# A recurrence before a router: state products moved behind the next scores, rank and logit products moved within the turn

## The chip, the cores and the metric

The kernel runs on one core of a Trainium2 chip. Its engines work side by side: TensorE (PE in the profile; its weight loads are PEld), VectorE (DVE), ScalarE (ACT), GpSimd (POOL), and the DMA queues that SyncE (SP) and GpSimd feed. Each engine takes its instructions in program order and waits for others through semaphores. The metric is the device time of one execution in microseconds (us).

## The reference

Two stages, all in float32. First a linear recurrence with decay (batch 4, 8 heads, 768 steps, 48 wide):

```python
for t in range(S):
    kt, vt, rt = (k[:, :, t], v[:, :, t], r[:, :, t])
    cur = np.einsum('bhd,bhe->bhde', u[None] * kt, vt)
    y[:, :, t] = np.einsum('bhd,bhde->bhe', rt, state + cur)
    state = w[None, :, :, None] * state + np.einsum('bhd,bhe->bhde', kt, vt)
```

Its output, as 3072 rows of 384 numbers, goes to a router with 8 experts: cosine logits of each row against 8 expert vectors, the best expert and its softmax weight, and then `gate * (relu(x @ w1[e]) @ w2[e])` with w1 384 x 1024 and w2 1024 x 384.

## The kernel before

The recurrence is done in chunks of 128 steps. A *unit* i is one chunk c of one batch row b (`c, b = divmod(i, 4)`), so there are 24 units, and one turn of the loop handles one unit, with parts of its neighbours. Four units make a *group* of the router. Within a chunk, y is the sum of three things: the state from before the chunk times r (`T`, `RT`), the masked scores within the chunk times v (`AT`, `V`), and the diagonal with u (`xd`, on ScalarE). Heads go in pairs, 48 rows each at partitions 0 and 64.

```python
def turn_r(k, i):      # TensorE: four transposes (rt), DVE: RT = rt * powers of the decay
def turn_k(k, i):      # TensorE: four transposes (kt), ScalarE: KT = copy of kt

def scores(k, i):
    RT, KT = k.RT[i], k.KT.pop(i)
    at = [k.ps.tile([128, NP, C], F32, name="at", tag="at") for _ in range(2)]
    for p in range(NP):
        for s in range(2):
            rows = slice(s * DP, s * DP + D)
            nc.tensor.matmul(at[s][:, p, :], KT[rows, p, :], RT[rows, p, :], start=True, stop=True)   # L388

def masked(k, i, s):   # DVE: AT[s] = at[s] * umask                                                   # L394
def states(k, i):      # TensorE: st = K^T V of this chunk                                            # L409
def carry(k, i):       # DVE, GpSimd: state += st, state *= decay of a chunk

def sums(k, i):
    ...
    y = [k.ps.tile([128, NP // 2, C], F32, name="y", tag="y") for _ in range(2)]
    for q in range(NP // 2):
        for u in range(2) if c > 0 else ():
            for s in range(2):
                p, n = 2 * q + u, (DP, D)[u]
                mm(                                                                                   # L443
                    y[s][u * DP : u * DP + n, q, :], T[s * DP : s * DP + D, p * D : p * D + n],
                    RT[s * DP : s * DP + D, p, :], start=(q == 0), stop=False, skip_group_check=True,
                )
    for s in range(2):
        for q in range(NP // 2):
            for u in range(2):
                ...
                mm(                                                                                   # L452
                    y[s][u * DP : u * DP + n, q, :], V[:, h * D : h * D + n], AT[s][:, p, :],
                    start=(c == 0 and q == 0), stop=True, skip_group_check=True,
                )
        yT = k.yT[i % len(k.yT)]
        nc.scalar.copy(yT[0:PP, s], y[s][0:PP])                                                       # L457

def rows(k, i):        # TensorE: four transposes of yT (yrows, L470), DVE: X = yrows + xd (L476)
def own_rows(k, i, half):  # ScalarE: four of the eight xd = V * diag (L346)
def turn_rows(k, g, b):    # TensorE: three transposes of X (xp, L556), ScalarE: xT = copy of xp (L558)
def squares(k, g, b):      # ScalarE: sum of squares of X (L563)
def logits(k, g):          # TensorE: lgT, 12 products with 32 columns (L572); needs the xT of four units
def logits_out(k, g):      # ScalarE: copy of lgT
def turn_logits(k, g):     # TensorE: one transpose (lg)
def ranks(k, g):           # TensorE: two products (rank, L625, L626); DVE reads them in places
def located(k, g):         # DVE: two small operations on what places gives
def taken(k, g):           # TensorE: four products (take, L718)
```

PSUM's eight banks are handed out by tag, in turn:

```python
HELD = {"tp": (0, 1), "at": (2, 3), "y": (4, 5), "st": (6,), "xp": (7,), "ps": (0, 1, 6, 7, 2, 3, 4, 5)}
```

rt, yrows, lgT and rank share the two banks of "tp"; each unit's y takes both banks of "y". The loop, cut to the steps that matter, in the order in which each engine gets them:

```python
for i in range(-1, units):
    ...
    whole(places, i - 4)           # whole(f, n): only when n is the last unit of a group
    whole(logits_out, i - 3)
    on(turn_r, i + 1)              # rt
    on(own_rows, i, 0)             # xd, first half
    on(turn_k, i + 1)              # kt, KT
    whole(turn_logits, i - 3)
    ...                            # scaled, own (GpSimd), squares, own_rows(i, 1), choose, before
    whole(located, i - 4)
    ...                            # gates, lanes, listed, own_sum
    on(sums, i)                    # L443, L452, yT
    on(states, i)                  # st
    whole(taken, i - 6, "xp")
    on(carry, i)
    on(scores, i + 1)              # at
    on(masked, i + 1, 0)
    on(rows, i)                    # yrows, X
    on(masked, i + 1, 1)
    of_group(put, i)               # X to memory
    of_group(turn_rows, i - 1)     # xp, xT
    whole(logits, i - 2)           # lgT
    whole(ranks, i - 3)            # rank
```

In the last turns two tiles of rows for the two smallest experts are gathered early (`Early`): the list for it is worked out on DVE, a gather on GpSimd brings the rows, and `turn` transposes them (early_x, L1025) after the last unit's sums. The rest of the experts follows as one long run of matmuls.

Of the kernel before, what the change touches and what calls it, by code (L numbers as in the profile page):

```python
# [10 lines left out]
F32 = mybir.dt.float32  # L11
# [6 lines left out]
B, H, S, D = 4, 8, 768, 48  # L18
DM, E, F = H * D, 8, 1024
N = B * S  # L20
C = 128
NCH = S // C
DP = 64
NP = H // 2
# [211 lines left out]
def build_experts(k):  # L236

    nc, pool = k.nc, k.aconst
    emb, tau = k.emb_rows, k.tau_rows
    sq = k.work.tile([E, DM], F32, name="emb_sq", tag="sq")  # L240
    nrm = pool.tile([E, 1], F32, name="emb_nrm")
    nc.scalar.activation(sq, emb, ACT.Square, accum_out=nrm)
    nc.gpsimd.tensor_tensor(out=nrm, in0=nrm, in1=k.half[0:E, 0:1], op=ALU.pow)
    nc.gpsimd.tensor_scalar(nrm, nrm, 1e-6, tau, ALU.add, ALU.mult)
    yield
    nc.vector.reciprocal(nrm, nrm)
    yield
    nc.scalar.mul(emb, emb, nrm)
    yield
    ps = k.ps.tile([128, NK, E], F32, name="ps", tag="xp")  # L250
    for c in range(NK):
        nc.tensor.transpose(ps[:, c, :], emb[:, c * 128 : (c + 1) * 128], k.ident[0:E, 0:E])
    nc.vector.tensor_copy(k.ent[:, :, 0:E], ps)
    yield
# [19 lines left out]
def load_w1(k, e, w1):  # L274
    k.nc.sync.dma_start(out=w1, in_=k.w1[bass.ds(e, 1)].rearrange("o (c p) f -> p (o c) f", p=128))
# [59 lines left out]
def own_sum(k, i):  # L335
    diag = k.work.tile([128, H], F32, name="diag", tag="diag")
    k.nc.vector.reduce_sum(diag, k.KU.pop(i), axis=AX.X)
    k.diag[i] = diag
# [53 lines left out]
def masked(k, i, s):  # L392
    a = k.work.tile([128, NP, C], F32, name=f"AT{s}", tag=f"AT{s}")
    k.nc.vector.tensor_mul(a, k.at[i][s], k.umask[:, None, :].to_broadcast([128, NP, C]))  # L394
    k.AT.setdefault(i, []).append(a)
# [29 lines left out]
    nc.gpsimd.tensor_mul(T[0:PP], T[0:PP], k.wC[0:PP])  # L425


def sums(k, i):

    nc = k.nc
    mm = nc.tensor.matmul
    c, b = divmod(i, B)
    V, RT, AT, T = k.loaded[i][2], k.RT.pop(i), k.AT.pop(i), k.state[b]
    V, T = (a.rearrange("q h d -> q (h d)") for a in (V, T))
    y = [k.ps.tile([128, NP // 2, C], F32, name="y", tag="y") for _ in range(2)]
    for q in range(NP // 2):
        for u in range(2) if c > 0 else ():  # L440
            for s in range(2):
                p, n = 2 * q + u, (DP, D)[u]
                mm(  # L443
                    y[s][u * DP : u * DP + n, q, :], T[s * DP : s * DP + D, p * D : p * D + n],
                    RT[s * DP : s * DP + D, p, :], start=(q == 0), stop=False, skip_group_check=True,
                )
    for s in range(2):
        for q in range(NP // 2):
            for u in range(2):
                p, n = 2 * q + u, DP if c == 0 and u == 0 else D  # L450
                h = 2 * p + s
# [6 lines that stand above are left out]
    if b == 0:  # L458
        k.groups[c] = group(k, c)
# [77 lines left out]
def group(k, c):  # L537

    g = Net()
    g.c = c  # L540
    g.X = k.rows.tile([128, B, DM], F32, name="X", tag="X")
    g.ssq = k.rt.tile([128, B], F32, name="ssq", tag="ssq")
    g.xT = {}
    return g
# [92 lines left out]
def norms(k, g):  # L637
    k.nc.gpsimd.tensor_tensor(out=g.ssq, in0=g.ssq, in1=k.half, op=ALU.pow)
# [72 lines left out]
def listed(k, g):  # L711
    g.what = chosen(k, g.c, g.sel)
# [134 lines left out]
def attention(k):  # L847


    units = B * NCH  # L850

    def on(f, i, *more):
        if 0 <= i < units:
            f(k, i, *more)

    def of_group(f, i):
        if 0 <= i < units:
            f(k, k.groups[i // B], i % B)

    def whole(f, i, *more):  # L860
        if 0 <= i < units and i % B == B - 1:
            f(k, k.groups[i // B], *more)

    emb, tables = build_experts(k), build_turned(k)
    for i in range(-1, units):
        j = i - SETTLED * B
        if 0 < i + AHEAD < units:
            load(k, i + AHEAD)
        whole(places, i - 4)
        whole(logits_out, i - 3)  # L870
        if i >= 0:
            on(turn_r, i + 1)
        if i == 0:
            own_sum(k, i)
        if B <= i < units - 1:
            on(own_rows, i, 0)
        if i >= 0:
            on(turn_k, i + 1)
        if 0 < i < B:
            own_rows(k, i, 0)  # L880
        whole(turn_logits, i - 3)
        if i == B + 3:
            norms(k, k.groups[0])
        on(scaled, i + 2)
        if i < 0:
            own_r(k, 0)
        on(own, i + 2)
        for n in SQUARES.get(i, (i - 1,)):
            of_group(squares, n)
        if B <= i < units - 1:  # L890
            on(own_rows, i, 1)
        if i > B + 1:
            whole(norms, i - 2)
        if j == 10:
            k.lists = turned_lists(k, perm, "tp")
            lists = taken_by_rank(k, k.lists)
            first = [Early(k, r, *lists, w) for r, w in zip(LAST, k.weights)]
        whole(choose, i - 3)
        whole(before, i - 3)
        whole(located, i - 4)  # L900
        whole(gates, i - 5)
        whole(lanes, i - 5)
        whole(listed, i - 5)
        if 0 <= i < units - 2:
            on(own_sum, i + 1)
        if j == 7:
            load_, count = loads(k, "xp")
        if j == 9:
            expert_of(k, by)
            number = expert_number(k, LAST[0])  # L910
            load_w1(k, number, k.weights[0][0])
        on(sums, i)
        on(states, i)
        for n in (0, 1) if i == 0 else (1,) if 0 < i < B else ():
            own_rows(k, i, n)
        whole(taken, i - 6, "xp")
        whole(exps, i - 4)
        on(carry, i)
        if 0 < i < B + 2:
            next(tables)  # L920
        whole(summed, i - 6)
        if i == B:
            next(emb)
        on(scores, i + 1)
        on(masked, i + 1, 0)
        if i == 0:
            masked(k, i + 1, 1)
        if i == units - 1:
            first[0].turn()
        on(rows, i)  # L930
        if i != 0:
            on(masked, i + 1, 1)
        if i == units - 2:
            own_sum(k, i + 1)
            own_rows_once(k, i + 1)
        of_group(put, i)
        if j == 10:
            load_w2(k, number, k.weights[0][1])
        of_group(turn_rows, i - 1)
        whole(logits, i - 2)  # L940
        whole(ranks, i - 3)
        if i == 0:
            build_constants(k)
        if i in (1, 2, 3):
            next(emb)
        if 3 <= i < 3 + len(k.ring):
            k.nc.gpsimd.memset(k.ring[i - 3], 0.0)
        if j == 8:
            by = order(k, load_)
        if j == 9:  # L950
            settle(k, by, count)
            perm = turner(k, by)


    g, h = k.groups[NCH - 2], k.groups[NCH - 1]
    early = itertools.chain(*(f.steps(lambda: to) for f in first))

    def fill(count):
        for _ in range(count):
            next(early, None)  # L960

    load_weights(k, expert_number(k, LAST[1]), k.weights[1])
    first[1].turn()
    fill(1)
    gates(k, g)
    lanes(k, g)
    listed(k, g)
    turn_rows(k, h, B - 1)
    squares(k, h, B - 1)
    norms(k, h)  # L970
    fill(1)
    logits(k, h)
    logits_out(k, h)
    fill(1)
    turn_logits(k, h)
    choose(k, h)
    before(k, h)
    to = outs(k, lists[0], E * TM)
    taken(k, g, "tp")
    fill(2)  # L980
    ranks(k, h)
    load_, _ = loads(k, "xp")
    places(k, h)
    exps(k, h)
    located(k, h)
    lanes(k, h)
    gates(k, h)
    listed(k, h)
    summed(k, g)
    by = order(k, load_, k.settled)  # L990
    perm = turner(k, by)
    fill(6)
    taken(k, h, "tp")
    summed(k, h)
    fill(1)
    lists = turned_lists(k, perm, "xp")
    k.take, k.gates = taken_by_rank(k, lists)
    k.rows_of = {r: gathers(k, r) for r in LAST}
    k.to = outs(k, k.take, E * TM)
    caps_passed(k, load_, by)  # L1000
    for _ in early:
        pass
# [615 lines left out]
```

## Time and profile before

The time before is 398.59 us, the median of 3 runs (398.39 to 399.5); the profiled execution has a span of 396.4 us, with the full clock granted to TensorE (0.997).

| engine | busy us | share of the span |
|---|---|---|
| TensorE matmuls | 386.9 | 98% |
| TensorE weight loads | 352.5 | 89% |
| VectorE | 253.2 | 64% |
| ScalarE | 173.1 | 44% |
| GpSimd | 160.9 | 41% |

The loop over the units takes roughly the first 131 us, the experts the rest. In the loop ScalarE is far busier than over the span: 7.0 to 8.0 us of each 10 us from 40 to 120 us.

How to read the lines: a line of the timeline gives the start in us, the duration from the first start to the last end, the engine, the line of the kernel, the operation, what is written from what, the shape (rows*columns of the array for matmuls), and how many records. In brackets stands the idle time of the engine just before it and what ended it. A float32 matmul is recorded as two passes, so eight products are sixteen records. Matmuls overlap by their pipeline depth: a group's first start to the next group's first start is the time that it takes. In the view of one tile, a line says which engine's instruction waited for it, for how long in sum, and how often.

### The profile page before, as it was taken

What the parts mean: (1) busy time and instruction counts of PE and PEld (TensorE: products, weight loads), DVE (VectorE), ACT (ScalarE), POOL (GpSimd) and SP (SyncE); (2) the same over time, 40 slices, a digit from 0 to 9 for tenths busy, and PEclk for the clock granted to TensorE, in tenths of its full rate; (3) what the DMA queues carried; (4) which work ended last, traced back from release to release, by engine and by line L of the source; (5) the groups of instructions that cost most, each with busy time, mean ns of one, the idle gap of its engine ahead of it and who ended that gap; (6) DMA issues with size and microseconds to landing.
All of it is one profiled execution on the core that took longest, in us unless ns stands there. A gap on an engine that the chain in (4) does not pass through costs nothing.

```text
span 396.4 us, 9266 instructions
## 1 busy us (share of the span) xinstructions
PE 386.9 (98%) x3542; PEld 352.5 (89%) x3542; DVE 253.2 (64%) x600; ACT 173.1 (44%) x524; POOL 160.9 (41%) x216
## 2 busy tenths in 40 slices
PE   7999999999999999999999999999999999999993
PEld 4988888889888877899999999999999999799783
DVE  6887878787788670757667668257275456655601
ACT  4887777777677412333333332233323243133120
POOL 7998796858664232500701502220350350200111
PEclk9999999999999999999999999999999999999998
DMA  7899887767606972244705532434164170150111
GB/s 146 163 215 214 189 180 162 157 136 149 142 33 206 288 285 65 87 161 163 255 7 215 196 106 94 133 112 161 55 227 159 43 237 3 40 180 0 41 39 44
DMA packets 93797, 54.35 MB, mean 137 GB/s; under 512 B 76938, under 2 KB 88381, under 8 KB 93747
## 3 DMA queue, kind: packets, MB, share of 16 engines
q1 hardware_dynamic: 90242, 44.26, 41.4%
q0 software_dynamic: 3296, 9.44, 7.3%
q8 instruction: 29, 0.48, 0.5%
q14 instruction: 22, 0.17, 0.1%
q10 hardware_dynamic: 208, 0.00, 0.0%
HBM read 44.45 MB, written 9.63 MB: 136 GB/s over the span
## 4 chain that ended last, share of the span: by engine, by line
PE 86%; SPq 4%; ACT 3%; DMA 2%; DVE 2%; POOL 1%; issue 1%; POOLq 0%; DVEq 0%; ACTq 0%
PE ps L1226 25%; PE ps L1290 18%; PE ps L1330 5%; PE at L388 4%; PE ps L1344 4%; PE y L452 4%; PE early_h L1036 3%; PE early_y L1045 3%; PE ps L1204 3%; PE yrows L470 2%; PE ps L1174 2%; PE y L443 2%; PE rt L360 2%; PE kt L369 2%; PE xp L556 2%; PE st L409 2%
## 5 line engine op out<-in xcount | busy, mean ns | idle before, releaser
L1090 POOL DMA_INDIRECT out_dram<-y,to x25 | 30.1, 1204 | 173.5 <-DVE Sh L1365 109.9
L1226 PE MATMUL ps<-xTe,w 128*128 128x192 f32 (+3 forms) x336 | 62.9, 327 | 0.0
L1226 PEld LDWEIGHTS ps<-xTe,w 128*128 128x128 f32 x336 | 55.9, 190 | 0.5
L346 ACT ACTIVATE xd<-V,diag 128x48 f32<-128x48 f32 x184 | 46.2, 326 | 0.1
L394 DVE TENSOR_TENSOR AT<-at,umask 128x512 f32<-128x512 f32 x48 | 32.7, 685 | 10.5 <-PE at L388 10.3
L1233 ACT ACTIVATE hT<-hT 128x384 f32<-128x384 f32 (+3 forms) x42 | 22.0, 523 | 32.4 <-DVE hT L1256 19.7
L1290 PE MATMUL ps<-Tw,Sh 128*128 128x192 f32 x192 | 32.5, 326 | 0.0
L1290 PEld LDWEIGHTS ps<-Tw,Sh 128*128 128x128 f32 x192 | 31.4, 190 | 0.0
L1081 POOL DMA_INDIRECT G<-xs,take x25 | 27.0, 1080 | 10.5 <-issue 4.6
L1226 PE MATMUL ps<-Tx,Sw 128*128 128x192 f32 (+3 forms) x168 | 29.7, 326 | 0.0
L388 PE MATMUL at<-RT,KT 48*128 48x128 f32 x384 | 27.9, 285 | 0.3 <-DVE RT L362 0.3
L1243 DVE TENSOR_TENSOR u<-ps,p 128x384 f32<-128x384 f32 (+3 forms) x14 | 7.8, 558 | 31.3 <-ACT p L1240 16.6
L1226 PEld LDWEIGHTS ps<-Tx,Sw 128*128 128x128 f32 x168 | 27.6, 190 | 0.1
L452 PE MATMUL y<-AT,V 128*48 128x128 f32 (+1 forms) x384 | 26.0, 278 | 0.0
L388 PEld LDWEIGHTS at<-RT,KT 48*128 48x128 f32 x384 | 23.3, 187 | 2.6 <-issue 0.7
L332 POOL TENSOR_TENSOR KU<-KU,Rpad 128x384 f32<-128x384 f32 x24 | 24.1, 1004 | 1.8
L452 PEld LDWEIGHTS y<-AT,V 128*48 128x48 f32 (+1 forms) x384 | 19.9, 124 | 4.2 <-issue 3.6
L1290 PE MATMUL ps<-w,hT 128*128 128x192 f32 x128 | 23.4, 326 | 0.0
L328 POOL TENSOR_TENSOR KU<-K,u_bc 128x384 f32<-128x384 f32 x23 | 23.2, 1008 | 0.0
L317 POOL TENSOR_TENSOR Kpad<-K,kpow 128x384 f32<-128x384 f32 x23 | 23.1, 1004 | 0.1
L558 ACT COPY xT<-xp 128x384 f32<-128x384 f32 x24 | 11.5, 479 | 25.5 <-PE xp L556 25.5
L1253 ACT ACTIVATE hT<-ps 128x384 f32<-128x384 f32 (+3 forms) x14 | 6.9, 490 | 35.7 <-PE ps L1226 35.7
(240 smaller groups left out, 816.5 us busy)
## 6 DMA issues: line engine op xcount, KB each, us to landing
w<-in_moe_w_dram SPq DMA_DIRECT2D x16, 1536.0 KB, 6.9
Rpad<-in_r_dram SPq DMA_DIRECT2D x24, 192.0 KB, 4.4
V<-in_v_dram SPq DMA_DIRECT2D x24, 192.0 KB, 4.2
xs<-X SPq DMA_DIRECT2D x24, 192.0 KB, 2.7
K<-in_k_dram SPq DMA_DIRECT2D x23, 192.0 KB, 3.7
G<-xs,take POOLq DMA_INDIRECT x27, 3.2
out_dram<-y,to POOLq DMA_INDIRECT x25, 3.5
Kpad<-in_k_dram SPq DMA_DIRECT2D x1, 192.0 KB, 3.2
```

What stands on the lines that cost most here:

```text
L317: k.nc.gpsimd.tensor_mul(k.Kpad[i % len(k.Kpad)][:, :, 0:D], k.loaded[i][0], k.kpow)
L328: k.nc.gpsimd.tensor_mul(k.KU[i], k.loaded[i][0], k.u_bc)
L332: k.nc.gpsimd.tensor_mul(k.KU[i], k.KU[i], k.loaded[i][1][:, :, 0:D])
L346: k.nc.scalar.mul(k.xd[i][:, h, :], V[:, h, :], diag[:, h : h + 1])
L388: nc.tensor.matmul(at[s][:, p, :], KT[rows, p, :], RT[rows, p, :], start=True, stop=True)
L394: k.nc.vector.tensor_mul(a, k.at[i][s], k.umask[:, None, :].to_broadcast([128, NP, C]))
L452: mm(y[s][u * DP : u * DP + n, q, :], V[:, h * D : h * D + n], AT[s][:, p, :], start=(c == 0 and q == 0), stop=True, skip_group_check=True,)
L1081: nc.gpsimd.indirect_dma_start(out=G[0:n, :], out_offset=None, in_=k.xs[:, :], in_offset=IndirectOffsetOnAxis(ap=take[0:n], axis=0), bound ...
L1090: put = k.nc.gpsimd.indirect_dma_start(out=k.out[:, :], out_offset=IndirectOffsetOnAxis(ap=to, axis=0), in_=y, in_offset=None, bounds_chec ...
L1226: nc.tensor.matmul(ps[:, j, :], weights[:, (f + j) * 128 : (f + j + 1) * 128], moving, start=(first and j == 0), stop=True, skip_group_che ...
L1233: nc.scalar.activation(h, h, ACT.Relu)
L1290: nc.tensor.matmul(ps, a[:, f, :], b[:, f, :], start=(first and f == 0), stop=(f == NF // 2 - 1), skip_group_check=True)
```

## The change

The products with the state are taken out of `sums` into a step of their own, `from_state`, which the loop runs for the next unit, right behind that unit's scores. The two have the same 48 rows, at partitions 0 and 64, and both read RT. The two masks then follow one another on DVE, ahead of the X of the unit before. The products for the ranks move from the end of a turn to the middle of the next turn, with the operations that read them; there the bank that they leave is not wanted at once. The logits move from the end of a turn to just in front of V's products of the same turn, both being products with 128 rows and few columns, and ScalarE's copy of them follows in the same turn. The same instructions are run, in another order.

```diff
-def sums(k, i):
+def from_state(k, i):
     c, b = divmod(i, B)
-    V, RT, AT, T = k.loaded[i][2], k.RT.pop(i), k.AT.pop(i), k.state[b]
-    V, T = (a.rearrange("q h d -> q (h d)") for a in (V, T))
-    y = [k.ps.tile([128, NP // 2, C], F32, name="y", tag="y") for _ in range(2)]
+    RT, T = k.RT.pop(i), k.state[b].rearrange("q h d -> q (h d)")
+    y = k.y[i] = [k.ps.tile([128, NP // 2, C], F32, name="y", tag="y") for _ in range(2)]
     for q in range(NP // 2):
         for u in range(2) if c > 0 else ():
             ...
+def sums(k, i):
+    V, AT, y = k.loaded[i][2].rearrange("q h d -> q (h d)"), k.AT.pop(i), k.y.pop(i)
     for s in range(2):
         ...
@@ the loop
-        whole(places, i - 4)
-        whole(logits_out, i - 3)
         ...
-        whole(located, i - 4)
         ...
             on(own_sum, i + 1)
+        for step in (ranks, places, located):
+            whole(step, i - 4)
         ...
+        whole(logits, i - 2)
         on(sums, i)
+        whole(logits_out, i - 2)
         on(states, i)
         ...
         on(scores, i + 1)
-        on(masked, i + 1, 0)
-        if i == 0:
-            masked(k, i + 1, 1)
+        on(from_state, i + 1)
+        for s in range(2):
+            on(masked, i + 1, s)
         ...
         on(rows, i)
-        if i != 0:
-            on(masked, i + 1, 1)
         ...
         of_group(turn_rows, i - 1)
-        whole(logits, i - 2)
-        whole(ranks, i - 3)
```

More of the change, by code (lines that the diff above doesn't have):

```diff
@@ L425, in carry @@
     nc.gpsimd.tensor_mul(T[0:PP], T[0:PP], k.wC[0:PP])
+def from_state(k, i):
+    c, b = divmod(i, B)
+    RT, T = k.RT.pop(i), k.state[b].rearrange("q h d -> q (h d)")
+    y = k.y[i] = [k.ps.tile([128, NP // 2, C], F32, name="y", tag="y") for _ in range(2)]
+    for q in range(NP // 2):
+        for u in range(2) if c > 0 else ():
+            for s in range(2):
+                p, n = 2 * q + u, (DP, D)[u]
+                k.nc.tensor.matmul(
+                    y[s][u * DP : u * DP + n, q, :], T[s * DP : s * DP + D, p * D : p * D + n],
+                    RT[s * DP : s * DP + D, p, :], start=(q == 0), stop=False, skip_group_check=True,
+                )
 def sums(k, i):
@@ L435, in sums @@
     c, b = divmod(i, B)
-    V, RT, AT, T = k.loaded[i][2], k.RT.pop(i), k.AT.pop(i), k.state[b]
-    V, T = (a.rearrange("q h d -> q (h d)") for a in (V, T))
-    y = [k.ps.tile([128, NP // 2, C], F32, name="y", tag="y") for _ in range(2)]
[L439 to L446, printed above, removed]
+    V, AT, y = k.loaded[i][2].rearrange("q h d -> q (h d)"), k.AT.pop(i), k.y.pop(i)
     for s in range(2):
@@ L924, in attention @@
         on(scores, i + 1)
-        on(masked, i + 1, 0)
-        if i == 0:
-            masked(k, i + 1, 1)
+        on(from_state, i + 1)
+        for s in range(2):
+            on(masked, i + 1, s)
         if i == units - 1:
```

## The prediction

> **What bounds the kernel now.** I read the busy shares first, then the stage by 10 us windows, then the timelines of TensorE and of ScalarE over one turn of the attention loop, and last the tile that ties the two together.
>
> The page says that TensorE is busy 98% of the span and weight loads 89%. So time is lost or won only where the chain on TensorE gets longer or shorter. The loop over the 24 units (one chunk of 128 steps of one batch row each) runs from about 8 to 131 us; the experts after it hang on its end.
>
> One plain turn, from the timelines of TensorE and its weight loads:
>
> ```profile
> 69.12 0.49 PE L556 MATMUL xp<-ident,X 128*128 128x128 f32 x3
> 69.45 0.60 PE L360 MATMUL rt<-ident,Rpad 128*128 128x128 f32 x4
> 69.89 0.60 PE L369 MATMUL kt<-ident,Kpad 128*128 128x128 f32 x4
> 70.42 0.66 PE L443 MATMUL y<-RT,state 48*64 48x128 f32 x16
> 71.00 1.08 PE L452 MATMUL y<-AT,V 128*48 128x128 f32 x16
> 71.91 0.61 PE L409 MATMUL st<-V,Kpad 128*64 128x48 f32 x16
> 72.46 1.16 PE L388 MATMUL at<-RT,KT 48*128 48x128 f32 x16
> 73.55 0.60 PE L470 MATMUL yrows<-ident,yT 112*128 112x112 f32 x4
> 73.99 0.49 PE L556 MATMUL xp<-ident,X 128*128 128x128 f32 x3
> ...
> 70.42 0.41 PEld L443 LDWEIGHTS y<-RT,state 48*64 48x64 f32 x16 [0.17 <-issue]
> 71.00 0.82 PEld L452 LDWEIGHTS y<-AT,V 128*48 128x48 f32 x16 [0.17 <-issue]
> ```
>
> The groups follow without a hole: from xp to xp is 73.99 - 69.12 = 4.87 us, and that is TensorE's own work. Before L443 (48*64) and L452 (128*48) the weight loads pause 0.17 us with nothing to wait for: the shape of the array changes there, as it does at L388 (48*128) and L470 (112*128). The same turn on ScalarE:
>
> ```profile
> 69.65 0.48 ACT L558 COPY xT<-xp 128x384 f32<-128x384 f32 x1 [1.34 <-PE xp L556]
> 70.03 1.01 ACT L346 ACTIVATE xd<-V,diag 128x48 f32<-128x48 f32 x4
> 70.94 0.56 ACT L378 COPY KT<-kt 128x512 f32<-128x512 f32 x1
> 71.40 0.53 ACT L563 ACTIVATE sq<-X 128x384 f32<-128x384 f32 x1
> 71.83 0.19 ACT L563 ACTIVATION_READ_ACCUMULATOR sq<-X 128x1 f32 x1
> 71.92 1.00 ACT L346 ACTIVATE xd<-V,diag 128x48 f32<-128x48 f32 x4
> 72.82 0.62 ACT L457 COPY yT<-y 112x256 f32<-112x256 f32 x2
> 74.52 0.48 ACT L558 COPY xT<-xp 128x384 f32<-128x384 f32 x1 [1.07 <-PE xp L556]
> ```
>
> ScalarE works without a hole from xT at 69.65 to the end of yT at 72.82 + 0.62 = 73.44: 3.79 us. Then it idles 1.07 us, until TensorE has done yrows (which reads yT) and xp (which stands behind yrows). So there is a ring: yT, then yrows and xp on TensorE, then xT and all the rest on ScalarE, then the next yT. Here yT ends at 73.44 and yrows starts at 73.55: the ring is only 0.1 us shorter than TensorE's own work. ScalarE is busy 78% of such a turn, and yet has nearly no room. Three turns already show it (the tile yT, who waited for it):
>
> ```profile
>   PEld yrows L470: 0.9, 3
> ```
>
> **What the Trainium skill says.** (1) "TensorEngine Tiling (Array Packing)", Key Properties: changing the tiling mode drains TensorE. The trace agrees: the first matmul of a new mode starts 0.20 us after the last one of the old, against 0.10 to 0.11 us inside a group, for each change here, also where only the columns change (xp to lgT, 0.20). (2) "TensorE: Matmul & The Clock Gate", the opening table: ScalarE's queue is strict FIFO. The trace agrees: xT is in front of xd, KT, sq and yT in every turn, and all of them lie idle while xT waits for xp. (3) "PSUM — Partial Sum Buffer", PSUM bank collisions raise a hardware error: a bank must be guarded by semaphores between engines. y has two banks and each unit takes both, so a product into y must wait until ScalarE has copied the y of the unit before. In the program as built, the moved products do carry a wait for ScalarE. (4) "Perfetto Trace Analysis", Optimizing Tensor Performance: matmul groups should rotate through PSUM banks so that evacuation of one lies beside the next. Here that rotation has a depth of one for y; no run so far shows more.
>
> **The change part by part.** No instruction is added or removed; TensorE's order changes, DVE and ScalarE move a few.
>
> *Products with the state (L443), from in front of V's products (L452) to behind the next scores (L388).* By modes: before kt, L443, L452, st, at, yrows has four changes (into 48*64, into 128*48, into 48*128 after st, into 112*128); after, kt, L452, st, at, L443, yrows has four again (into 128*48, 48*128, 48*64, 112*128). At 0.14 us each (0.20 instead of 0.11, and about 0.05 for the weights that could not be loaded ahead) that is a gain of nothing, unless a change of columns alone between at and L443 costs nothing, which xp to lgT speaks against.
>
> By waits: L443 of unit i+1 now writes y right after the scores, and so waits for both copies yT of unit i. And it stands between yT and yrows. The ring gets longer: yT end to first L443 0.05 (as at yrows where it waited, 116.7), L443 0.39, change 0.20, yrows 0.34, xp 0.10 + 0.22, last xp start to xT 0.31 (69.34 to 69.65): 1.61 us, and ScalarE's 3.79: 5.40 us. Before it was 1.61 - 0.39 - 0.20 = 1.02 and 3.79: 4.81. TensorE's work stays 4.87. So a plain turn goes from 4.87 to 5.40: +0.53.
>
> *Logits in front of V's products.* Before, xp, lgT, rt costs two changes of mode; after, kt, lgT, L452 replaces the change kt to L452, so one less: 0.14 per group of four units. ScalarE's copy of lgT moves into its idle time. The turn with lgT (0.79 more) and take (0.45 more) is 4.87 + 0.79 + 0.45 = 6.11 on TensorE, longer than the ring.
>
> *Ranks a turn later.* Before, rt behind the rank products starts 0.30 us after the last of them and goes on at 0.165 instead of 0.11: it waits for a bank that DVE's X add frees. That is 0.47 - 0.22 = 0.25 us per group; it goes away. After, the turn with ranks has 4.87 + 0.36 = 5.23 on TensorE, below the ring's 5.40.
>
> *One group of four turns, steady.* Before (starts of L443 at 48.83 and 70.42, 91.999, ...): 21.58 us. After: 6.11 + 3 x 5.40 = 22.31. So +0.73 per group, with the savings of ranks and logits counted in: without the ring they would have given -0.39.
>
> *The sum.* I place y443 of unit 4 where yrows of unit 3 stood (24.94) and compare each later one with the yrows of the unit before.
> - Units 4, 5, 6: ScalarE has two squares instead of one (and emb), passes of 4.80, 4.30, 4.30, with 1.60 each: 6.40, 5.90, 5.90, ending at 43.14 against 41.62: +1.5. Unit 7: 5.40 against 5.48: +1.4 in sum.
> - Units 8 to 19: three groups, +0.69 each by the exact starts (66.93 against 64.87): +3.5 in sum.
> - Unit 20 (no st any more): 5.40 against 4.55: +4.3. Unit 21, TensorE-bound with lgT (4.38 + 0.79 + 0.43 = 5.60) against 4.93: +5.0; part of that is lgT moved forward, and would come back in unit 22.
> - It does not come back: early_x at 130.79 waits for a gather, whose list is worked out on DVE behind the scores of unit 22 (at ends 121.5, gather issued 125.60, landed 130.65). That chain starts +5.0 late, so early_x stands at 135.8, and TensorE, ready at about 134.7, waits some 1.1 us there instead of 0.6.
> From early_x to the end TensorE is full and unchanged: +5.0 us, 398.6 to 403.6. I take 403.4, as a few small waits may overlap.
>
> **The rivals.**
> A. *Only TensorE counts, and the change does what it is for.* For it: TensorE 98% busy, ScalarE only 44% of the span and with an idle time of over 1 us each turn. Then 4 rank waits x 0.25 and 5 logits x 0.14 give -1.7 us: 396.9; part lost again at the gather, which would then come last: 397.8. Against it: that idle time is itself a wait for TensorE, and the margin of yT is 0.1 us in the plain turns (0.5 in those with more on TensorE).
> B. *The change from at to L443 is free, as both have rows of 48.* Then 20 x 0.14 = 2.8 us more would be saved: 395. Against it: xp to lgT shares its rows too, and pays 0.20. And with the ring last, TensorE's saving is worth nothing in three turns of four.
> C. *DVE becomes the bound*: the X add now stands behind both masks, and yrows comes later. DVE is 4.68 of 4.87 us busy in the fullest turn (69.65 to 74.52). A turn of 5.40 leaves it 0.7 us, so I hold it off the path; if RT came late for the scores, some 0.2 us per turn more: up to 407.
> D. *ScalarE's pass gets shorter*: y is ready earlier, but yT waits for ScalarE's own queue, not for y (its products end at about 72 us, yT starts at 72.82). No gain.
>
> **Range and chances.** The main term, 0.53 to 0.7 us for some 14 turns, rests on two intervals measured in the trace and on one wait that is in the program. What is unsure is the start (+-1), the tail (+-1) and C. Predicted 403.4 us, 400.5 to 406.5 eight times in ten. Two per cent faster (390.6) is beyond even B: 0.02. Two per cent slower (406.6) needs C or a longer tail: 0.10. Within 2%: 0.88.
>
> **What would show it.** In the profile after: L443's weight loads wait for ACT yT, about 0.5 us in three turns of four, where before yrows waited three times in all; a plain turn of 5.4 us; ScalarE's idle before xT rises from 1.07 to about 1.6 us; no wait at rt behind ranks; lgT with one pause less; early_x later by about 5 us, and the experts as long as before. I am wrong if plain turns stay at 4.87 (then yT is not waited for, A or B), or if the waits before L443 name DVE (C).

## The result, and the profile after

The changed kernel takes 403.02 us (median; 402.74 to 403.27), against 398.59 before. The ratio is 1.0109, 95% interval 1.0094 to 1.0123: it is slower by 1.1%, or 4.4 us. The profiled execution has a span of 401.0 us against 396.4, and the engines' counts of instructions are the same.

The busy shares hardly show it. From the page after:

```profile
PE 389.8 (97%) x3542; PEld 354.7 (88%) x3542; DVE 253.5 (63%) x600; ACT 171.9 (43%) x524; POOL 162.2 (40%) x216
```

TensorE has 2.9 us more recorded as busy, and every share went down a point. It is the single turn that tells. The timeline of TensorE after, one plain turn (no logits, ranks or take in it); L440 is what L443 was, L457 was L452, L475 was L470, L561 was L556:

```profile
72.09 0.49 PE L561 MATMUL xp<-ident,X 128*128 128x128 f32 x3
72.42 0.60 PE L360 MATMUL rt<-ident,Rpad 128*128 128x128 f32 x4
72.85 0.60 PE L369 MATMUL kt<-ident,Kpad 128*128 128x128 f32 x4
73.38 1.08 PE L457 MATMUL y<-AT,V 128*48 128x128 f32 x16
74.52 0.67 PE L409 MATMUL st<-V,Kpad 128*64 128x48 f32 x16
75.12 1.16 PE L388 MATMUL at<-RT,KT 48*128 48x128 f32 x16
76.21 0.90 PE L440 MATMUL y<-RT,state 48*64 48x128 f32 x16
77.04 0.60 PE L475 MATMUL yrows<-ident,yT 112*128 112x112 f32 x4
77.48 0.49 PE L561 MATMUL xp<-ident,X 128*128 128x128 f32 x3
```

From xp to xp is 77.48 - 72.09 = 5.39 us, where it was 4.87. Subtract the starts: from L457 to st are 1.14 us (0.91 before), and from L440 to yrows 0.83 us, where the state products before took 0.58. These two places hold the 0.5 us. The same stretch on ScalarE:

```profile
72.62 0.48 ACT L563 COPY xT<-xp 128x384 f32<-128x384 f32 x1 [1.47 <-PE xp L561]
72.99 1.01 ACT L346 ACTIVATE xd<-V,diag 128x48 f32<-128x48 f32 x4
73.91 0.57 ACT L378 COPY KT<-kt 128x512 f32<-128x512 f32 x1
74.37 0.53 ACT L568 ACTIVATE sq<-X 128x384 f32<-128x384 f32 x1
...
75.79 0.62 ACT L462 COPY yT<-y 112x256 f32<-112x256 f32 x2
78.01 0.48 ACT L563 COPY xT<-xp 128x384 f32<-128x384 f32 x1 [1.60 <-PE xp L561]
```

ScalarE's pass is what it was: 72.62 to 75.79 + 0.62 = 76.41, 3.79 us. Then it idles 1.60 us where it idled 1.07, waiting for TensorE, while TensorE waits for it: L440 starts at 76.21, but its second product needs the bank whose copy yT ends at 76.41, and only from there does it run through. Two engines that wait for each other in turn are both idle part of the time. The weight loads of TensorE show the other place:

```profile
74.52 0.54 PEld L409 LDWEIGHTS st<-V,Kpad 128*64 128x64 f32 x16 [0.31 <-ACT KT L378]
75.12 0.97 PEld L388 LDWEIGHTS at<-RT,KT 48*128 48x128 f32 x16
76.21 0.66 PEld L440 LDWEIGHTS y<-RT,state 48*64 48x64 f32 x16
77.04 0.39 PEld L475 LDWEIGHTS yrows<-ident,yT 112*128 112x128 f32 x4 [0.17 <-issue]
```

st waits for KT: kt and st share the one bank of "st", so st can't be written before ScalarE has read kt. KT ends at 73.91 + 0.57 = 74.48, st starts at 74.52. In the kernel before, KT ended 0.4 us ahead of st. A wait inside L440 has no bracket: it falls on its second product, and most of the idle time is covered by the weight loads of the first. Over the whole program the view of waits names, for these weight loads, only

```profile
PEld st L409 <- ACT KT L378: 2.6, 8, 0.8
PEld y L440 <- ACT yT L462: 1.6, 3, 0.7
```

eight and three times, although the starts of the products show one or both waits clearly in 13 of the 20 turns with state products. Where waits are short and the engine works ahead, compare starts, not brackets.

The turns side by side, each from the start of one xp to the next, in us, in the middle of the loop (one group; "take" is the turn whose scores follow the take products):

| turn | before | after |
|---|---|---|
| plain | 4.87 | 5.39 |
| take (after: with the logits) | 5.32 | 6.11 |
| next (before: with the logits) | 5.92 | 5.39 |
| ranks | 5.48 | 5.40 |
| group | 21.59 | 22.29 |

### The profile page after: what moved, and what is told of

Same layout as the page of the kernel before. It is cut to its first block, busy times and chain, and to the rows that moved or that the text cites. A ratio compares the mean times of both kernels' runs of the same rounds, so it can differ in the third digit from the quotient of the medians.

```text
span 401.0 us, 9262 instructions
## 1 busy us (share of the span) xinstructions
PE 389.8 (97%) x3542; PEld 354.7 (88%) x3542; DVE 253.5 (63%) x600; ACT 171.9 (43%) x524; POOL 162.2 (40%) x216
## 4 chain that ended last, share of the span: by engine, by line
PE 89%; ACT 4%; DVE 2%; DMA 1%; issue 1%; SPq 1%; POOL 0%; POOLq 0%; DVEq 0%; ACTq 0%
PE ps L1228 25%; PE ps L1292 18%; PE ps L1332 5%; PE at L388 5%; PE y L457 4%; PE ps L1346 4%; PE y L440 3%; PE early_h L1038 3%; PE yrows L475 3%; PE early_y L1047 3%; PE ps L1206 3%; PE ps L1176 2%; PE st L409 2%; ACT xd L346 2%; PE rt L360 2%; PE xp L561 2%
## 5 line engine op out<-in xcount | busy, mean ns | idle before, releaser
L394 DVE TENSOR_TENSOR AT<-at,umask 128x512 f32<-128x512 f32 x48 | 30.9, 686 | 9.1 <-PE at L388 8.9
L1083 POOL DMA_INDIRECT G<-xs,take x25 | 28.2, 1128 | 10.5 <-issue 4.3
L457 PE MATMUL y<-AT,V 128*48 128x128 f32 (+1 forms) x384 | 26.0, 277 | 0.0
L457 PEld LDWEIGHTS y<-AT,V 128*48 128x48 f32 (+1 forms) x384 | 19.9, 124 | 3.4 <-issue 2.7
```

Of the source, the lines that this page charges most:

```text
L457: mm(y[s][u * DP : u * DP + n, q, :], V[:, h * D : h * D + n], AT[s][:, p, :], start=(c == 0 and q == 0), stop=True, skip_group_check=True,)
L1083: nc.gpsimd.indirect_dma_start(out=G[0:n, :], out_offset=None, in_=k.xs[:, :], in_offset=IndirectOffsetOnAxis(ap=take[0:n], axis=0), bound ...
```

## The experiments

Two theories to be told apart. *The ring*: yT on ScalarE, then TensorE through yrows and xp, then xT at the head of ScalarE's queue and its whole pass to the next yT; the state products now stand inside it and make it 5.40 us, longer than TensorE's 4.87. *The order*: the new places cost or save on TensorE itself (changes of mode, banks), and ScalarE, with over 1 us idle per turn, doesn't count. Each ratio is to the kernel before on the same chip, with its 95% interval.

### E1: ranks and logits alone

The kernel before, with these two moves of the change and not the state products:

```diff
-        whole(places, i - 4)
-        whole(logits_out, i - 3)
-        whole(located, i - 4)
+        for step in (ranks, places, located):
+            whole(step, i - 4)
+        whole(logits, i - 2)
         on(sums, i)
+        whole(logits_out, i - 2)
-        whole(logits, i - 2)
-        whole(ranks, i - 3)
```

> Only the ranks and the logits are moved; the state products stay in front of V's products. Ring theory (the lost time is ScalarE's ring through y, and only the state products lengthen it): no ring here, and the two moves bring what was worked out for them, 4 rank waits x 0.25 us and 5 logits x 0.14 us = 1.7 us, of which about half is given back at the gather of the early rows: 397.7 us, with rt no longer waiting behind the rank products. Rival (any shift of these products costs, because TensorE or DVE waits elsewhere): 399 us or more.

Measured: ratio 0.9978 (0.9969 to 0.9987). The turn with ranks takes 5.23 instead of 5.48, so the 0.25 us wait is gone; the two turns in which the logits stand before and after sum to 6.11 + 4.97 = 11.08 instead of 11.24, so one change of mode (0.16) is saved. The plain turn is unchanged. The moves do what they are meant for, 0.4 us per group. Part is given back at the end of the loop, where the view of waits shows TensorE waiting 1.2 us for the list of the early rows:

```profile
PEld lists L805 <- DVE perm L799: 1.2, 1, 1.2
```

### E2: the state products alone

```diff
         on(scores, i + 1)
-        on(masked, i + 1, 0)
-        if i == 0:
-            masked(k, i + 1, 1)
+        on(from_state, i + 1)
+        for s in range(2):
+            on(masked, i + 1, s)
         ...
         on(rows, i)
-        if i != 0:
-            on(masked, i + 1, 1)
```

with `sums` split as in the change.

> Only the state products are moved behind the next scores (with the two masks in a row); ranks and logits stay at the end of a turn. Ring theory: plain turns of 5.40 us, turns with ranks or logits at their end 5.6 to 6.0, since KT and the copy of lgT then stand inside ScalarE's pass; 22.4 us per group of four: 403.5 us, so that the two other moves are worth next to nothing once the ring is last. Rival (TensorE's own order costs, the parts add up): after plus what ranks and logits saved, 404.7 us.

Measured: ratio 1.0165 (1.0151 to 1.0179), more than either expected. The plain turn is 5.39, as the ring says. But the group is 5.39 + 5.60 + 6.01 + 5.61 = 22.61 where 22.4 was expected, and the miss in the group is the turn with take:

```profile
57.77 0.83 PEld L457 LDWEIGHTS y<-AT,V 128*48 128x48 f32 x16 [0.17 <-issue]
58.91 0.48 PEld L409 LDWEIGHTS st<-V,Kpad 128*64 128x64 f32 x15 [0.32 <-ACT KT L378]
```

st waits for KT, and after that wait st, take, the scores, the state products, yrows and xp follow without another hole until xT, xd and KT come round again: a second ring, which leaves yT out, and which take makes longer by 0.45 us. In the changed kernel the logits stand in front of L457 in that very turn, and KT is done 0.6 us before st by then. So the moves of ranks and logits are worth more on top of the state products (from 1.0165 to 1.0109) than alone (0.9978), not next to nothing, as the expectation had it: they also take the copy of the logits, and the wait of kt behind the ranks, out of ScalarE's pass, which with them takes 4.40 and 4.01 us instead of 3.79; with 1.60 on TensorE that is the 6.00 and 5.61 of these turns. Both theories had summed too simply. The group's excess of 0.2 us, 0.6 us over three groups, is only part of the miss (1.0165, where 403.5 us stood for 1.0123). Two other turns with the logits took 6.51 and 6.22 us instead of 6.0; the rest was not taken apart.

### E3: the changed kernel, with part of ScalarE's work moved into its idle time

```diff
-        if B <= i < units - 1:
-            on(own_rows, i, 0)            # in front: xT
         ...
         on(sums, i)
         whole(logits_out, i - 2)
+        if B <= i + 1 < units - 1:
+            on(own_rows, i + 1, 0)        # behind: xT
```

> The changed kernel, with one thing moved on ScalarE: the first four xd of the next unit are issued right behind yT, in front of xT, where ScalarE lay idle. Ring theory: 0.92 us of ScalarE's pass now lies beside the state products, yrows and xp on TensorE; the ring falls from 5.40 to about 4.5 us, below TensorE's 4.87, no wait for yT is left, plain turns are 4.87 us again, and the time is that of ranks and logits alone: 397.7 us. Rival (the place of the state products costs TensorE itself, by modes or banks): stays at 403 us.

Measured: ratio 0.9986 (0.998 to 0.9993). With every matmul at the place of the changed kernel, four instructions per turn of another engine take away the whole loss. That decides for the ring. The plain turn is 5.00, though, where 4.87 was expected (and 0.9978 in all), and some wait for yT is left: L440 to yrows takes 0.71 us. ScalarE's timeline there (a plain turn of E3) says why:

```profile
49.26 0.48 ACT L563 COPY xT<-xp 128x384 f32<-128x384 f32 x1 [0.81 <-PE xp L561]
50.13 0.59 ACT L378 COPY KT<-kt 128x512 f32<-128x512 f32 x1 [0.40 <-PE kt L369]
50.62 0.53 ACT L568 ACTIVATE sq<-X 128x384 f32<-128x384 f32 x1
...
52.03 0.62 ACT L462 COPY yT<-y 112x256 f32<-112x256 f32 x2
53.01 1.01 ACT L346 ACTIVATE xd<-V,diag 128x48 f32<-128x48 f32 x4 [0.35 <-ACT yT L462]
54.26 0.48 ACT L563 COPY xT<-xp 128x384 f32<-128x384 f32 x1 [0.24 <-PE xp L561]
```

Now ScalarE waits for kt (0.40) before KT, and KT, sq, xd and yT hang on that: a third ring, through kt.

### E4: the same move in the kernel before

> The kernel before with the same move of xd on ScalarE. Ring theory: there the ring (4.81 us) was below TensorE's 4.87 in nearly all turns; only the three turns where yrows waited for yT (0.9 us in sum) get shorter: 398.0 us. Rival (xd in front of xT is a gain by itself, whatever the order of TensorE): as much as in e3, about 393 us.

Measured: ratio 1.0003 (0.9994 to 1.0011): no gain, so the move is worth something only where the ring is last: the four turns of a group stay at 4.87, 5.32, 5.92 and 5.48. The small gain that was expected did arise in the turns where yrows had waited (4.87 instead of 5.13, 4.42 instead of 4.62), and was lost in one other turn, 6.90 instead of 5.92. There the chain of waits leads through DVE:

```profile
35.74 0.86 DVE tie L213
36.60 0.11 issue
36.71 1.76 DVE X L476
38.47 0.08 DVE AT L394
38.55 0.02 issue
38.57 0.66 PE rt L360 x4
```

The small operation at L213 (128x8) started at 35.66 and took 2.81 us; in the kernel before it took 0.16. What held it is told at the end, as far as it can be.

### E5: E3, with the squares in front of KT

```diff
+        for n in SQUARES.get(i, (i - 1,)):
+            of_group(squares, n)
         if i >= 0:
             on(turn_k, i + 1)             # KT
-        for n in SQUARES.get(i, (i - 1,)):
-            of_group(squares, n)
```

> As e3, and ScalarE's squares are also moved in front of KT, into the 0.4 us in which ScalarE waited for kt there. Ring theory, now with a second ring through kt: in e3 yT still came 0.13 us late in one turn of four, because the way xp, rt, kt, KT, sq, xd, yT, state products, yrows, xp takes 5.00 us; without sq in it, it takes about 4.7, below TensorE's 4.87: turns of 4.87 instead of 5.00, some 0.8 us in all, ratio to before 0.9965. Rival (those turns are long for TensorE's own sake): ratio 0.9986 as in e3.

Measured: ratio 0.9968 (0.9956 to 0.9981), as expected. The plain turn is 4.87:

```profile
72.25 0.61 PE L409 MATMUL st<-V,Kpad 128*64 128x48 f32 x16
72.79 1.16 PE L388 MATMUL at<-RT,KT 48*128 48x128 f32 x16
73.88 0.65 PE L440 MATMUL y<-RT,state 48*64 48x128 f32 x16
74.47 0.60 PE L475 MATMUL yrows<-ident,yT 112*128 112x112 f32 x4
```

L440 to yrows is 0.59 again (0.83 in the changed kernel). The four turns of a group, 4.87, 6.11, 4.98 and 5.23, are those of E1 to 0.01 us. So with the rings out of the way the place of the state products is worth nothing to TensorE, for good or ill.

### E6: E1, with the last group left as it was

`logits` of turn 21 and `ranks` of turn 22, with what reads them, stay at the end of their turns (`LATE = units - 3`; the moved forms run only for earlier turns):

```diff
+        if i < LATE:
+            whole(logits, i - 2)
         on(sums, i)
+        if i < LATE:
+            whole(logits_out, i - 2)
         ...
+        if i >= LATE:
+            whole(logits, i - 2)
+            whole(ranks, i - 3)
```

> e1 (ranks and logits moved, state products not), but the last group's logits (turn 21) and ranks (turn 22) stay at the end of their turns as before, so that the list of the early rows is begun earlier. If half of the gain of e1 was given back at the lists and at the early rows (there TensorE waits 1.2 us for the list): about 0.7 us less than e1, ratio to before 0.996. If what limits there is elsewhere: as e1, 0.9978.

Measured: ratio 0.9956 (0.9942 to 0.997). By the ratios that is 0.9 us less than E1, where 0.7 was expected; in the two traces the early rows are transposed 0.5 us sooner, at 130.03 us against 130.55. So what E1 gave back is gained here, and its size is known only roughly: the two intervals touch.

### E7 and E8: less and more work for ScalarE

E7 is the changed kernel with the squares summed over 8 of 384 columns (`g.X[:, b, 0:8]`); it leaves out most of the norm, so its gates are other numbers. E8 is the kernel before, with the squares of units 6 to 21 taken twice.

> The changed kernel, with the squares taken over 8 of the 384 columns (the gates come out different, the routing does not): 0.23 us less on ScalarE per turn, 0.46 in the turns with two. Ring theory: plain turns 5.17 instead of 5.40, turns with ranks 5.23, the turn with the logits 6.11 as before; some 3 to 3.5 us less than the changed kernel, ratio to before 1.0025. Rival (ScalarE is busy only 43% and has idle time in each turn, so its work does not count): 1.0109 as the changed kernel.

> The kernel before, with the squares of units 6 to 21 done twice: 0.52 us more on ScalarE per turn. Ring theory: its ring was 4.81, and becomes 5.33 against TensorE's 4.87; plain turns 5.33, the turn with take 5.33, the others nearly as they were: +0.55 us per group and the last turns, 3.4 us in all, ratio 1.0085. Rival (ScalarE idles over 1 us per turn, and takes it in): 1.000.

Measured: E7 1.0017 (1.001 to 1.0025), plain turns 5.15, with ranks 5.23, with the logits 6.11. E8 1.0055 (1.0039 to 1.0071), plain turns 5.28. Both go as the ring says per turn, 0.24 us off and 0.41 us on; "ScalarE idles, so its work doesn't count" falls twice. In E8 the size was overestimated (1.0085): the new ring is 5.28 and not 5.33, and a group grows by 0.42 us (22.00 against 21.58), not by 0.55, since only the plain turn is below the new ring; the turn with take was at 5.32 already and stayed. One early turn of E8 (6.39 instead of 5.92) is long for the reason met in E4, not for the ring. The wait that the ring makes, from E8's view of waits, was 0.9 us in sum and 3 times before:

```profile
PEld yrows L470 <- ACT yT L457: 3.3, 7, 0.9
PE yrows L470 <- ACT yT L457: 1.8, 5, 0.7
```

### E9 and E10: all of it together, with and without the state products' move

E9 joins E5 and E6; E10 is the same without the state products' move.

> All of it together: the changed kernel with xd and the squares moved on ScalarE (e5) and the last group's logits and ranks left at the end of their turns (e6). Ring theory, with the rings below TensorE's work everywhere: the state products' new place is then worth nothing either way, and this is e6 within 0.3 us: ratio 0.9956. Rival (the new place saves a change of mode, 0.14 us in each of 20 turns, once the ring is out of the way): 2.8 us less, 0.989.

> The same without the state products' move: e6 with xd and the squares moved on ScalarE. Ring theory: e6 had the ring last in two turns only (of units 4 and 20, 0.5 us in sum); ratio 0.9945 to 0.9956, the same as e9 within 0.3 us.

Measured: E9 0.9956 (0.9942 to 0.9969), E10 0.9959 (0.9946 to 0.9973): not to be told apart, nor from E6. That settles the state products: no gain of a mode change hides behind the ring. E6, the simplest of the three, beats both kernels, by 0.4% against the one before.

## Why the prediction was right

- *A plain turn from 4.87 to 5.40 by the ring.* Right: 5.39. That it is the ring and not TensorE's order is shown by E3 and E5 (ScalarE's order alone brings 4.87 back) and by E7 and E8 (ScalarE's work moves the turn, in either kernel).
- *The turn with logits and take at 6.11, the group at 22.31.* Right: 6.11 and 22.29. E1 shows the two parts of the saving by themselves, 0.25 for the ranks and 0.16 for the logits against 0.25 and 0.14.
- *The start, passes of 6.40, 5.90 and 5.90.* Right to 0.01 us.
- *Four changes of mode before and four after, so no gain there (against rival B).* Right: from the last product of the scores to the first of L440, which share their rows, it took 0.20 us, and E9 and E10 do not differ. The working said 0.20 us for each change; the one from st to the scores takes 0.15 (72.31 to 72.46), in both kernels alike, so the count stands.
- *Early rows 5.0 us later, 1.1 us of wait there.* The delay is slightly off: 135.38 against 130.79, 4.6 us later. The gather was issued 5.2 us later (130.81 against 125.60), but TensorE went on 4.6 us after that, where it had been 5.2. The wait is wrong: from the last product of V, TensorE stood 0.5 us longer than inside the group (134.77 to 135.38), not 1.1; it had been 0.6. From the early rows to the end both executions take 265.6 us, so the experts are as long as before, as forecast. The 0.4 us are most of what lies between the sum, 403.6, and 403.02; that the stated 403.4 is closer still is an allowance for overlaps that the working does not derive.
- *L443 waits 0.5 us for yT.* Right in its sum and half wrong in its place: 0.23 us of it fall on st, which waits for KT through the shared bank, and 0.25 on the state products. That rt, yrows, lgT and rank share banks was known beforehand; that kt and st do was not looked at. In the changed kernel it made no difference to the sum, since KT is in the same pass of ScalarE; in E2 it did.
- *Rival A* was right in what it said of TensorE and wrong as a forecast: its 396.9 to 397.8 is what E1 reaches, without the ring. *Rival C* (DVE) did not come: no turn is above 5.40 without logits in the middle of the loop. *Rival D* (yT is held by ScalarE's own queue, so an earlier y gains nothing) is borne out: in the plain turn after, the last of V's products starts at 74.19 and yT at 75.79, directly behind xd, and E3, which shortens exactly that queue, brings yT forward.

## What to carry to other kernels

Before moving work on a saturated engine across a point where it hands over to another, follow the loop of waits all the way round and add its durations: here 3.79 us of ScalarE and 1.02 of TensorE made 4.81 against 4.87, and putting 0.59 us of matmuls into it made the loop the bound, though ScalarE was 44% busy over the program (6.7 to 7.9 us of each 10 us from 40 to 120 us, a little less than the range given at the start). Idle time in front of an instruction that heads an in-order queue is no spare time unless something can be put in front of it; four instructions moved there were worth the whole loss. And a move that pays by itself is best tried by itself: two of the three parts of this change were gains.

## What the runs showed of the hardware that was not expected

- A very small DVE operation took 17 times as long in two of the twelve traces. L213 (TENSOR_SCALAR, 128x8) took 0.16 us in ten of them, where it started while GpSimd stood between two operations. In E4 (2.81 us) and E8 (2.84 us) it started while GpSimd was at work, and ended 0.03 us after GpSimd's run of operations without a gap: 38.47 after 38.44 in E4, 38.60 after 38.58 in E8. DVE's next ones, issued behind it, show long times of their own (1.76 for X instead of 0.56). It is not every operation of DVE: in the kernel before, a mask and X ran in 0.69 and 0.56 us beside such a run of GpSimd (34.90 to 37.70). The times fit L213 waiting for a gap of GpSimd, but no run took GpSimd's work away there, so this stays open.
- From issue to first use, the same gather of early rows took 5.2 us before and 4.6 us after. The difference is in the transfer: it landed 5.05 us after its issue before and 4.43 after. Why is open.
